# Retention and feed-forward on one core: more loads in flight, weight tiles of the beginning in two loads, and a new fixed order of the beginning

## The chip, the core and the metric

The kernel runs on one core of one Trainium2 chip. A core has five engines with an instruction stream each: TensorE (PE, with its weight loads as PEld), VectorE (DVE), ScalarE (ACT), GpSimd (POOL) and SyncE (SP), which here issues loads and stores only. Engines wait for each other and for DMA transfers by semaphores; each works through its own list in order. The metric is device time in microseconds (us). The kernel before takes 577.41 us, the median of three runs (575.93, 577.41, 577.48).

## The reference, cut to what matters

```python
# q, k, v: (4, 8, 768, 64)
for t in range(S):
    state = gamma * state + outer(k[t], v[t])        # per batch and head
    y[t] = scale * q[t] @ state
x = y.transpose(0, 2, 1, 3).reshape(3072, 512)
h = x @ w_in                                          # 512 x 2048
g = h * clip(h + 3, 0, 6) / 6
out = g @ w_out                                       # 2048 x 512
```

All inputs and the output are float32.

## The kernel before, in words

The 3072 tokens are 24 rows of 128 tokens, six to a batch. Four rows make a unit u of 512 tokens. The recurrence is computed in chunks of 64 tokens: scores of a row (k times q), weighed by a mask or a decay, times v, plus q times the state before, and the state is moved on by k times v. The result x of a unit is split into a high and a low part in a reduced float32 format, and so are the weights; a product is then three matmuls (high by high, high by low, low by high).

w_in is 16 tiles of 128 columns (j), each 128 x 512 in 64-bit floats, that is 512 KB. VectorE and ScalarE convert a tile to float32 in six steps and split it: a, b (bits of the exponent and the mantissa), e (ScalarE), q, f (the last that reads the loaded tile), w, and then u (high part, ScalarE) and v (low part, VectorE). A product tile hu.j is 12 matmuls of 128 x 512 (four k blocks by three). ScalarE (r) and VectorE (g) turn it into g, which goes to a buffer in HBM. When all units are through, a second phase multiplies by w_out with seven products in place of eight.

Up to the products of units 0 and 1 with all 16 tiles the order on each engine is written by hand: HEAD (L56), a list of words that `step` (L539 on) turns into instructions one by one. Each engine does its own words in this order; how the engines stand to each other is left to the semaphores. A word is a letter and numbers:

- Lr: the loads of row r (kt, qt, vn, kn of 256 KB each; from row 8 on also dq). F: the load of the next weight tile, F0 to F15 in this text. Both go to SyncE.
- O, N, Y, U (rows 0 to 3) and s, S, i, p, y (rows 4 to 7), P, Q (rows 8 on): scores, inner products, products with the state, sums of the state, all on TensorE. T: small table products. zn: n matmuls that fill time and whose result is not used.
- m: weighing the scores; x: the scaled result of a row; l: its low part (VectorE); X: its high part, A, B, J, K: copies of the state (ScalarE); c, d: decay of v (GpSimd for rows 0 to 5, ScalarE for 6 and 7); C: copies of the tables.
- a, b, e, q, f, w, u, v followed by the tile's number; hu.j: three of the 12 matmuls of a product tile; ru.j and gu.j.

SyncE's loads of the beginning go through `read` (L151). It keeps a list of loads in flight with their bytes per partition (2 KB for a row load, 4 KB for a weight tile). Where a new load would exceed the limit FLYING, the oldest are dropped from the list and the new one waits until the last dropped one has landed. This holds up to row 7; row 8 and later loads wait only for their buffers.

```python
    FLYING = 10 << 10
    ...
        while flying and sum(n for n, _ in flying) + size > FLYING:
            after = flying.pop(0)[1]
```

A weight tile is loaded into one of two buffers (tag st), so F of tile n also waits for step f of tile n - 2. The first product of unit 0 needs x of rows 0 to 3, of unit 1 x of rows 4 to 7.

Of the kernel before, what the change touches and what calls it, by code (L numbers as in the profile page):

```python
# [31 lines left out]
def retention_ffn(ctx: ExitStack, tc: tile.TileContext, qkv, w_in, w_out, dvs, dkc, dqc, dmc, tab, out, B, H, S, D):  # L32
# [23 lines left out]
    HEAD = """  # L56
        L0 L1 F L2 L3 L4 L5 F O0 T0 m0.0 c0 T1 C0 T2 m0.1 d0 C1 T3 C2 N0 C3 U0 x0 c1 T4 B0 d1 O1 C4 X0 l0 Y1 m1.0 U1
        m1.1 T5 B1 a0 N1 C5 e0 c2 b0 O2 d2 f0 x1 Y2 m2.0 X1 U2 m2.1 l1 B2 O3 q0 F L6 L7 c3 N2 d3 w0 Y3 u0 m3.1 m3.0 U3
        c4 x2 N3 B3 d4 v0 X2 s4 x3 p4 l2 X3 c5 m4 A4 d5 l3 S5 a1 y4 b1 e1 q1 B4 f1 F z1 h0.0 w1 p5 x4 u1 h0.0 m5 A5 X4
        v1 h0.0 c6 l4 S6 a2 d6 b2 y5 m6 h0.0 e2 x5 h0.1 q2 c7 h0.1 f2 F r0.0 p6 w2 d7 h0.1 g0.0 h0.1 a3 A6 u2 b3 S7 q3  # L60
        r0.1 v2 e3 y6 m7 X5 h0.2 f3 B6 h0.2 w3 p7 l5 i7 u3 x6 h0.2 A7 g0.1 y7 X6 v3 h0.2 B7 l6 h0.3 r0.2 x7 h0.3 g0.2
        X7 h0.3 a4 l7 L8 F h0.3 e4 b4 h1.0 r0.3 q4 h1.0 g0.3 h1.0 f4 F h1.0 w4 h1.1 r1.0 h1.1 u4 g1.0 h1.1 v4 h1.1
        h1.2 r1.1 Q8 g1.1 a5 h1.2 b5 K8 m8 e5 P9 q5 h0.4 J9 f5 F L9 h0.4 w5 h0.4 a6 u5 h0.4 b6 e6 q6 h1.2 r0.4 v5 h1.2
        f6 F h1.3 r1.2 w6 h1.3 a7 u6 h1.3 g1.2 e7 h1.3 b7 v6 h1.4 r1.3 f7 h1.4 g0.4 h1.4 g1.3 h1.4 q7 h1.5 r1.4 w7
        h1.5 a8 u7 g1.4 h1.5 e8 v7 h1.5 f8 Q9 L10 F r1.5 b8 q8 F g1.5 h1.6 K9 m9 X8 h1.6 w8 h1.6 l8 u8 h1.6 v8 h1.7
        r1.6 h1.7 g1.6 h1.7 h1.7 P10 r1.7 h1.8 J10 g1.7 h1.8 a9 b9 h1.8 e9 q9 h1.8 f9 F Q10 r1.8 w9 g1.8 u9 a10 h0.5
        K10 v9 X9 h0.5 m10 e10 h0.5 l9 h0.5 b10 q10 h0.6 r0.5 f10 F h0.6 g0.5 h0.6 w10 h0.6 a11 u10 b11 P11 r0.6 q11
        h1.9 J11 v10 e11 h1.9 g0.6 h1.9 f11 F h1.9 w11 h1.10 r1.9 a12 b12 h1.10 u11 g1.9 e12 h1.10 q12 h1.10 f12 F L11
        h0.7 r1.10 v11 h0.7 w12 h0.7 g1.10 u12 h0.7 a13 v12 e13 h0.8 b13 r0.7 h0.8 f13 h0.8 g0.7 q13 F h0.8 w13 h0.9
        r0.8 a14 h0.9 u13 g0.8 h0.9 e14 b14 q14 h0.9 f14 h0.10 r0.9 v13 h0.10 g0.9 h0.10 w14 h0.10 a15 u14 Q11 L12 b15  # L70
        r0.10 q15 e15 v14 h0.11 g0.10 K11 X10 h0.11 m11 l10 h0.11 f15 h0.11 w15 h0.12 r0.11 h0.12 u15 g0.11 h0.12 v15
        h0.12 h0.13 r0.12 h0.13 g0.12 h0.13 h0.13 h0.14 r0.13 h0.14 g0.13 h0.14 h0.14 h0.15 r0.14 h0.15 g0.14 h0.15
        h0.15 P12 r0.15 h1.11 J12 g0.15 h1.11 h1.11 h1.11 Q12 r1.11 g1.11 h1.12 m12 K12 X11 h1.12 l11 h1.12 h1.12
        h1.13 r1.12 h1.13 g1.12 h1.13 h1.13 h1.14 r1.13 h1.14 g1.13 h1.14 h1.14 h1.15 r1.14 h1.15 g1.14 h1.15 h1.15
        r1.15 g1.15
    """
# [827 lines left out]
```

## Time and profile before

| | before |
|---|---|
| median of three runs | 577.41 us |
| the profiled execution | 577.87 us, span 576.2 us |
| TensorE busy | 564.4 us, 98% of the span, 4930 matmuls |
| VectorE busy | 425.6 us, 74% |
| ScalarE busy | 242.6 us, 42% |
| GpSimd busy | 49.0 us, 9% |
| granted TensorE clock | full in every slice |
| chain that ended last | TensorE 91%, DMA 6%, VectorE 1% |

The span is the time between the first and the last instruction of the program in the profile; the execution's own time is a little more. Busy times are those in which an engine has an instruction at work; a busy TensorE can still be waiting inside, since the ends of matmuls are modelled. The chain is followed back from the last instruction, at each step to what released it. The whole DMA share of it lies in the beginning.

### The profile page before, as it was taken

To read this page: it belongs to the slowest core of one execution; us is meant where nothing else is said; L and a number is where in the kernel's file an instruction comes from. 1 tells how busy PE (TensorE), PEld (TensorE's weight loads), DVE (VectorE), ACT (ScalarE), POOL (GpSimd) and SP (SyncE) were. 2 spreads that over 40 slices of the span, in tenths; PEclk is the share of its full clock that TensorE was granted. 3 is DMA by queue.
4 is the path that set the end of the run, shared out by engine and by line. 5 is a ranking of instruction groups with operands and counts; after the bars stand their busy time and mean duration, and the time that the engine had idled before them with its cause. 6 is when DMAs were issued, how large, how long until landed. Compare 5 with 4: busy or idle time off the path is not lost.

```text
span 576.2 us, 12026 instructions
## 1 busy us (share of the span) xinstructions
PE 564.4 (98%) x4930; PEld 460.9 (80%) x4930; DVE 425.6 (74%) x594; ACT 242.6 (42%) x356; POOL 49.0 (9%) x58
## 2 busy tenths in 40 slices
PE   8789999999999999999999999999999999999997
PEld 6667888888888888888888888888888888888885
DVE  6688879942577767777737989689776798767881
ACT  3274445432444344444424654543335443444430
POOL 3301110121111111222000000000000000000000
PEclk9999999999999999999999999999999999999999
DMA  7986685844666666676443384665744757545611
GB/s 247 291 277 218 203 275 203 292 172 167 202 220 207 210 236 228 212 241 250 167 160 120 147 301 164 196 205 183 251 151 144 234 166 243 200 127 176 208 73 74
DMA packets 58467, 115.82 MB, mean 201 GB/s; under 512 B 5926, under 2 KB 6822, under 8 KB 58412
## 3 DMA queue, kind: packets, MB, share of 16 engines
q1 hardware_dynamic: 44144, 89.67, 47.8%
q10 hardware_dynamic: 14268, 25.38, 11.5%
q8 instruction: 39, 0.64, 0.5%
q14 instruction: 16, 0.13, 0.1%
HBM read 83.57 MB, written 31.46 MB: 200 GB/s over the span
## 4 chain that ended last, share of the span: by engine, by line
PE 91%; DMA 6%; DVE 1%; SPq 0%; issue 0%; DVEq 0%
PE h L497 45%; PE o L774 40%; DMA early<-in_qkv 4%; DMA st<-in_w_in 3%; PE uz L450 2%; PE sc L450 2%; PE y L450 2%; SPq L153 0%; DVE w L216 0%; DVE xr L601 0%; DVE x L216 0%; DVE g L508 0%; DVE we L177 0%; DVE wb L189 0%; DVE kept_v L718 0%
## 5 line engine op out<-in xcount | busy, mean ns | idle before, releaser
L497 PE MATMUL h<-x,w 128*128 128x512 f32 x1152 | 270.4, 393 | 0.5 <-DVE x L216 0.4
L497 PEld LDWEIGHTS h<-x,w 128*128 128x128 f32 x1152 | 214.0, 188 | 46.8 <-DVE x L216 0.8
L774 PE MATMUL o<-gc,w 128*128 128x512 f32 x1008 | 231.7, 391 | 0.0
L774 PEld LDWEIGHTS o<-gc,w 128*128 128x128 f32 x1008 | 188.9, 187 | 42.6
L504 ACT ACTIVATE g<-h,three 128x512 f32<-128x512 f32 x96 | 65.9, 688 | 109.2 <-PE h L497 82.2
L508 DVE SCALAR_TENSOR_TENSOR g<-g,h 128x512 f32<-128x512 f32 x96 | 65.8, 685 | 61.9 <-ACT g L504 61.6
L213 ACT ACTIVATE gc<-gv 128x1024 fp32r<-128x1024 f32 x48 | 50.9, 1060 | 62.2 <-PE o L774 58.1
L216 DVE TENSOR_TENSOR gc<-gv,gc 128x1024 fp32r<-128x1024 f32 x48 | 58.6, 1222 | 24.9 <-ACT gc L213 24.9
L213 ACT ACTIVATE gc<-spare 128x1024 fp32r<-128x1024 f32 x36 | 38.2, 1061 | 51.6 <-PE o L774 39.2
L216 DVE TENSOR_TENSOR gc<-spare,gc 128x1024 fp32r<-128x1024 f32 x36 | 44.0, 1221 | 11.2 <-ACT gc L213 11.1
L186 ACT ACTIVATE we<-we,ebias 128x512 int32<-128x512 int32 x32 | 23.0, 720 | 21.6 <-DVE we L177 21.6
L213 ACT ACTIVATE w<-ww 128x384 fp32r<-128x384 f32 (+2 forms) x34 | 18.6, 552 | 26.0 <-DVE ww L200 25.3
L454 ACT ACTIVATE state<-uz 128x256 f32<-128x256 f32 x41 | 15.6, 380 | 21.7 <-PE y L450 10.5
L200 DVE SCALAR_TENSOR_TENSOR ww<-wb,we 128x512 f32<-128x512 f32 x32 | 23.4, 733 | 0.9
L189 DVE SCALAR_TENSOR_TENSOR wb<-st,wb 128x512 f32<-128x512 uint32 x32 | 22.7, 708 | 0.7
L339 POOL TENSOR_TENSOR qs<-qt,dq 128x512 f32<-128x512 f32 x16 | 22.4, 1398 | 8.4 <-DMA dq<-in_decays_q 7.2
L194 DVE SCALAR_TENSOR_TENSOR we<-st,we 128x512 int32<-128x512 int32 x32 | 23.0, 720 | 0.0
L216 DVE TENSOR_TENSOR w<-ww,w 128x384 fp32r<-128x384 f32 (+2 forms) x34 | 21.0, 623 | 0.7 <-ACT w L213 0.5
L132 DVE TENSOR_TENSOR spare<-spare,gv 128x1024 f32<-128x1024 f32 x12 | 14.7, 1222 | 5.5 <-DMA gv<-gd 5.4
L450 PE MATMUL y<-qs,state 64*64 64x64 f32 x480 | 18.3, 222 | 0.0
L177 DVE TENSOR_SCALAR we<-st 128x512 int32<-128x512 int32 x32 | 13.6, 426 | 6.3 <-DMA st<-in_w_in 6.0
L450 PE MATMUL y<-am,vn 64*64 64x64 f32 x512 | 18.2, 219 | 0.0
(71 smaller groups left out, 408.1 us busy)
## 6 DMA issues: line engine op xcount, KB each, us to landing
gd<-g ACTq DMA_DIRECT2D x96, 256.0 KB, 2.9
gv<-gd SPq DMA_DIRECT2D x48, 512.0 KB, 4.9
gv<-gd SPq DMA_DIRECT2D x48, 256.0 KB, 3.1
st<-in_w_in SPq DMA_DIRECT2D x16, 512.0 KB, 4.5
st<-in_w_out SPq DMA_DIRECT2D x16, 512.0 KB, 5.9
early<-in_qkv SPq DMA_DIRECT2D x28, 256.0 KB, 4.2
kt<-in_qkv SPq DMA_DIRECT2D x16, 256.0 KB, 3.6
qt<-in_qkv SPq DMA_DIRECT2D x16, 256.0 KB, 4.0
```

The source lines that it names most:

```text
L186: nc.scalar.activation(out=t["e"], in_=t["e"], func=AF.Relu, scale=8.0, bias=ebias)
L189: nc.vector.scalar_tensor_tensor(out=t["b"].bitcast(F32), in0=lo.bitcast(U32), scalar=2.0**-32, in1=t["b"], op0=ALU.mult, op1=ALU.add)
L194: nc.vector.scalar_tensor_tensor(out=t["e"], in0=hi, scalar=-2147483648, in1=t["e"], op0=ALU.bitwise_and, op1=ALU.bitwise_or)
L200: nc.vector.scalar_tensor_tensor(out=t["w"], in0=t["b"].bitcast(F32), scalar=2.0**-20, in1=t["e"].bitcast(F32), op0=ALU.mult, op1=ALU.mult)
L213: nc.scalar.activation(out=hi, in_=src, func=AF.Copy)
L216: nc.vector.tensor_tensor(out=lo, in0=src, in1=hi, op=ALU.subtract)
L339: nc.gpsimd.tensor_tensor(out=t["qs"], in0=t["qt"], in1=d, op=ALU.mult)
L450: nc.tensor.matmul(out_, lhs, rhs, start=start, stop=True, skip_group_check=True)
L497: nc.tensor.matmul(h, t[:, o, a], xs[u][b][:, k], start=k + n == 0, stop=(k, n) == (NK - 1, 2), skip_group_check=True)
L504: return g, nc.scalar.activation(out=g, in_=h, func=AF.Relu, bias=three).ins
L508: ins = nc.vector.scalar_tensor_tensor(out=g, in0=g, scalar=6.0, in1=h, op0=ALU.min, op1=ALU.mult)
L774: nc.tensor.matmul(acc[i][h] if last else acc[i][:, h], w2c[j][:, RIGHT[i], x, h], gc[:, y, jj], start=j == 0 and n == 0, stop=j == NFP - ...
```

## The change

Three edits. The limit of bytes in flight goes from 10 KB to 14 KB per partition, that is from five row loads to seven (1.25 to 1.75 MB). In the beginning a weight tile is read by two loads of 2 KB per partition into the two halves of its buffer; the weight tiles of w_out in the later part are still one load. The list HEAD has another order; it has the same words, but for z1, which is now z4.

```diff
-    FLYING = 10 << 10
+    FLYING = 14 << 10
...
-        L0 L1 F L2 L3 L4 L5 F O0 T0 m0.0 c0 T1 C0 T2 m0.1 d0 C1 T3 C2 N0 C3 U0 x0 c1 T4 B0 d1 O1 C4 X0 l0 Y1 m1.0 U1
...
+        L0 F L1 L2 F L3 L4 L5 O0 c0 T0 m0.1 T1 d0 C0 T2 m0.0 C1 U0 C2 N0 B0 a0 b0 e0 q0 T3 T4 T5 f0 F L6 O1 c1 C3 Y1
...
-    def fetch(src):
+    def fetch(src, parts=1):
         st = wst.tile([P, src.shape[-1]], I64, tag="st", name=nm("st"), bufs=2)
-        read(st, src)
+        n = src.shape[-1] // parts
+        for i in range(parts):
+            read(st[:, i * n : (i + 1) * n], src[:, i * n : (i + 1) * n])
         return st
...
-                fetched.append(fetch(w_in[len(fetched)]))
+                fetched.append(fetch(w_in[len(fetched)], 2))
```

SyncE at the program's begin, before: early and kn are row loads (rows 0 and 1 in early_3, 2 and 3 in early_6, 4 and 5 in early_8, 6 and 7 in early_26; kn is the fourth load of an odd row), st is a weight tile, kt_66 on is row 8.

```order
L153 DMA early_3_134<-in_qkv 128x512 x7
L153 DMA kn_4_142<-in_qkv 128x512
L153 DMA st_5_144<-in_w_in 128x512
L153 DMA early_6_146<-in_qkv 128x512 x7
L153 DMA kn_7_154<-in_qkv 128x512
L153 DMA early_8_156<-in_qkv 128x512 x7
L153 DMA kn_9_164<-in_qkv 128x256
L153 DMA st_10_166<-in_w_in 128x512
L153 DMA st_25_340<-in_w_in 128x512
L153 DMA early_26_342<-in_qkv 128x512 x7
L153 DMA kn_27_350<-in_qkv 128x512
L153 DMA st_37_499<-in_w_in 128x512
```

Behind these rows come one more weight tile (st_48_613) and then row 8 (kt_66_802). Now, from the begin on, the same engine; early_9 is rows 4 and 5, early_21 rows 6 and 7:

```order
L153 DMA early_3_134<-in_qkv 128x512 x4
L153 DMA st_4_139<-in_w_in 128x256 x2
L153 DMA early_3_134<-in_qkv 128x512 x3
L153 DMA early_6_147<-in_qkv 128x512 x4
L153 DMA st_7_152<-in_w_in 128x256 x2
L153 DMA early_6_147<-in_qkv 128x512 x3
L153 DMA early_9_160<-in_qkv 128x512 x7
L153 DMA st_20_230<-in_w_in 128x256 x2
L153 DMA early_21_233<-in_qkv 128x512 x4
L153 DMA st_35_444<-in_w_in 128x256 x2
L153 DMA st_40_511<-in_w_in 128x256 x2
L153 DMA early_21_233<-in_qkv 128x512 x3
```

The single loads kn between these rows are left out. The first tile moved ahead of row 1, the second ahead of row 3, and the fourth and fifth ahead of row 7; three more tiles (st_52, st_63, st_75) now stand behind row 7 and ahead of row 8 (kt_76_856), where one stood before.

TensorE at the end of the attention of row 7, before: y_2 and uz are the last sums of that row, h_55 is the product tile h0.2, h_62 is h0.3, h_74 h1.0, h_78 h1.1 and h_80 h1.2; x_18 is x of unit 0, x_43 of unit 1; sc_125 is the scores of row 8.

```order
L450 MATMUL y_2_133<-early_26_342,state_60_754 64x64 x2
L497 MATMUL h_55_701<-x_18_241,w1_29_364 128x512 x3
L497 MATMUL h_62_782<-x_18_241,w1_29_364 128x512 x6
L497 MATMUL h_62_782<-x_18_241,w1_58_713 128x512 x6
L497 MATMUL h_74_824<-x_43_534,w1_29_364 128x512 x12
L497 MATMUL h_78_847<-x_43_534,w1_29_364 128x512 x12
L497 MATMUL h_80_866<-x_43_534,w1_29_364 128x512 x3
L450 MATMUL sc_125<-qt_67_804,kt_66_802 64x64 x16
```

Now: h_66 is h0.3, h_71 h0.4, h_74 h1.0, h_86 h1.1, h_91 h1.2; x_26 is x of unit 0, x_48 of unit 1.

```order
L452 MATMUL y_2_133<-early_21_233,state_65_786 64x64 x2
L499 MATMUL h_66_788<-x_26_311,w1_24_280 128x512 x3
L499 MATMUL h_66_788<-x_26_311,w1_55_636 128x512 x6
L499 MATMUL h_71_831<-x_26_311,w1_55_636 128x512 x9
L499 MATMUL h_74_848<-x_48_603,w1_24_280 128x512 x9
L499 MATMUL h_71_831<-x_26_311,w1_55_636 128x512 x3
L499 MATMUL h_74_848<-x_48_603,w1_24_280 128x512 x3
L499 MATMUL h_86_895<-x_48_603,w1_24_280 128x512 x12
L499 MATMUL h_91_920<-x_48_603,w1_24_280 128x512 x12
L452 MATMUL sc_125<-qt_77_858,kt_76_856 64x64 x16
```

A product tile of the fifth weight tile, h0.4, moved ahead of the first product tile of unit 1; before, it stood behind the scores of row 8. The scores of row 8 stand 48 products behind the begin of h0.4, and stood 27 behind the begin of h1.0.

VectorE at the same place, now: w1_55 is the low part of weight tiles (v), x_48 the low part of x of unit 1 (l), st_52 the sixth weight tile, g_64 and g_72 the results of h0.2 and h0.3.

```order
L510 SCALAR_TENSOR_TENSOR g_64_766<-g_64_766,h_57_653 128x512
L202 SCALAR_TENSOR_TENSOR ww_67_809<-wb_59_660,we_56_651 128x512
L603 TENSOR_TENSOR xr_69_816<-y_2_133,early_0_131 128x512
L179 TENSOR_SCALAR we_70_822<-st_52_626 128x512
L218 TENSOR_TENSOR w1_55_636<-ww_67_809,w1_55_636 128x4x128
L218 TENSOR_TENSOR x_48_603<-xr_69_816,x_48_603 128x4x128
L183 TENSOR_SCALAR wb_73_838<-st_52_626 128x512
L191 SCALAR_TENSOR_TENSOR wb_73_838<-st_52_626,wb_73_838 128x512
L510 SCALAR_TENSOR_TENSOR g_72_835<-g_72_835,h_66_788 128x512
L196 SCALAR_TENSOR_TENSOR we_70_822<-st_52_626,we_70_822 128x512
```

Before, the last low part of x of unit 1 (l7) stood behind the first step of tile 4 (a4), and the other steps of that tile behind l7; now all steps of tile 4 are ahead of l7, and step f of tile 5, which frees a buffer for the eighth tile, is the fifth instruction behind v of tile 4.

## Rows read from the trace of the kernel before

**Rows 1.** Busy time of each engine by stretches: the stretch, its length, busy time and instructions of PE, PEld, DVE, ACT and POOL, the granted clock, the DMA engines' busy share and GB/s.

```profile
2.00:42.00 40.00, 33.61 (x733) 26.25 (x731) 28.74 (x51) 17.93 (x44) 8.52 (x16) 1.00 0.88 285
6.16:50.46 44.30, 37.67 (x809) 29.34 (x807) 36.29 (x62) 21.01 (x50) 9.65 (x14) 1.00 0.84 276
60.00:140.00 80.00, 80.00 (x775) 65.18 (x774) 57.98 (x98) 34.22 (x60) 12.25 (x10) 1.00 0.67 230
```

**Rows 2.** The chain of waits in order of time, from the begin to 60 us: start, duration, what (early is a row load, st a weight tile).

```profile
2.65 4.37 DMA early<-in_qkv
7.04 5.90 DMA st<-in_w_in
...
25.71 4.11 DMA st<-in_w_in
...
35.30 4.45 DMA st<-in_w_in
...
39.84 0.43 DVE we L177
...
49.86 0.61 DVE x L216
50.52 6.19 PE h L497 x26
56.70 1.08 PE sc L450 x32
```

**Rows 3.** What SyncE's queue waited for, from 2 to 42 us: total us, times, longest.

```profile
SPq L153 <- DMA early<-in_qkv: 13.8, 19, 1.8
SPq L153 <- DMA st<-in_w_in: 6.8, 4, 3.2
```

**Rows 4.** Busy time by short stretches, columns as in rows 1: one with a full queue of loads, and three single microseconds.

```profile
3.00:8.00 5.00, 4.67 (x54) 3.07 (x55) 1.84 (x4) 1.08 (x2) 1.37 (x3) 1.00 1.04 342
13.00:14.00 1.00, 0.12 (x3) 0.00 (x0) 1.00 (x3) 0.52 (x1) 0.00 (x0) 1.00 0.19 68
...
25.00:26.00 1.00, 0.55 (x34) 0.45 (x32) 1.00 (x2) 0.39 (x1) 0.29 (x1) 1.00 0.50 130
...
38.00:39.00 1.00, 1.00 (x8) 0.84 (x5) 0.69 (x1) 1.00 (x5) 0.00 (x0) 1.00 0.80 152
```

**Rows 5.** VectorE's groups of instructions from 6.16 to 50.46 us: busy time, mean ns, and the idle time before them with what ended it. (The 3.6 us put down to "issue" lie before 6.16 us.)

```profile
L601 DVE TENSOR_TENSOR xr<-y,early 128x512 f32<-128x512 f32 x8 | 5.5, 687 | 1.2 <-PE y L450 1.2
...
L373 DVE TENSOR_TENSOR am<-sc,mask 128x512 f32<-128x512 f32 x8 | 5.1, 684 | 5.4 <-issue 3.6 <-PE y L450 1.9
...
L177 DVE TENSOR_SCALAR we<-st 128x512 int32<-128x512 int32 x5 | 2.2, 449 | 4.3 <-DMA st<-in_w_in 4.3
```

**Rows 6.** VectorE in order of time, 57 to 63 us, steps of two weight tiles: L177 is a, L181 b, L189 q, L194 f, L200 w, L216 v; start, duration.

```profile
57.39 0.42 DVE L177 TENSOR_SCALAR we<-st 128x512 int32<-128x512 int32 x1
57.73 0.42 DVE L181 TENSOR_SCALAR wb<-st 128x512 int32<-128x512 int32 x1
58.06 0.68 DVE L418 TENSOR_TENSOR am<-sc,cmask 128x512 f32<-128x512 f32 x1
58.66 0.68 DVE L189 SCALAR_TENSOR_TENSOR wb<-st,wb 128x512 f32<-128x512 uint32 x1
59.38 0.69 DVE L194 SCALAR_TENSOR_TENSOR we<-st,we 128x512 int32<-128x512 int32 x1
60.11 0.69 DVE L200 SCALAR_TENSOR_TENSOR ww<-wb,we 128x512 f32<-128x512 f32 x1
60.84 0.43 DVE L177 TENSOR_SCALAR we<-st 128x512 int32<-128x512 int32 x1
...
62.25 0.68 DVE L216 TENSOR_TENSOR w<-ww,w 128x512 fp32r<-128x512 f32 x1
62.85 0.68 DVE L194 SCALAR_TENSOR_TENSOR we<-st,we 128x512 int32<-128x512 int32 x1
```

**Rows 7.** TensorE: one filling matmul (z1, two records) and the first products behind it, in order of time; and 54 products in a row, from the chain.

```profile
27.91 0.70 PE L562 MATMUL h<-mask 128*128 128x256 f32 x2
28.25 1.06 PE L497 MATMUL h<-x,w 128*128 128x512 f32 x3
...
59.77 12.48 PE h L497 x54
```

**Rows 8.** Loads of a row from the ninth on: SyncE's issues of row 8 (its first) and at 60 us, in order of time; median time to landing of loads between 60 and 72 us; and GpSimd's scaling of row 8's kn.

```profile
37.57 0.42 SPq L153 DMA_DIRECT2D kt<-in_qkv  x1
...
60.10 0.33 SPq L153 DMA_DIRECT2D st<-in_w_in  x1
60.54 1.55 SPq L153 DMA_DIRECT2D kt<-in_qkv  x1
...
63.08 0.43 SPq L153 DMA_DIRECT2D am<-in_qkv  x1
...
64.14 0.65 SPq L153 DMA_DIRECT2D st<-in_w_in  x1
...
kt<-in_qkv SPq DMA_DIRECT2D x1, 256.0 KB, 5.5
...
am<-in_qkv SPq DMA_DIRECT2D x1, 256.0 KB, 6.2
...
46.11 1.21 POOL L335 TENSOR_TENSOR kn<-kn,ccst 128x512 f32<-128x512 f32 x1 [18.97 <-DMA kn<-in_qkv]
```

More of the change, by code (lines that the diff above doesn't have):

```diff
@@ L56, in retention_ffn @@
     HEAD = """
-        L0 L1 F L2 L3 L4 L5 F O0 T0 m0.0 c0 T1 C0 T2 m0.1 d0 C1 T3 C2 N0 C3 U0 x0 c1 T4 B0 d1 O1 C4 X0 l0 Y1 m1.0 U1
[L58 to L75, printed above, removed]
+        L0 F L1 L2 F L3 L4 L5 O0 c0 T0 m0.1 T1 d0 C0 T2 m0.0 C1 U0 C2 N0 B0 a0 b0 e0 q0 T3 T4 T5 f0 F L6 O1 c1 C3 Y1
+        d1 C4 m1.1 U1 m1.0 B1 w0 N1 c2 x0 u0 d2 O2 C5 X0 x1 U2 m2.0 X1 Y2 m2.1 B2 l0 N2 v0 c3 l1 O3 d3 x2 Y3 m3.0 X2
@@ new lines, in retention_ffn @@
+        m3.1 U3 l2 s4 B3 c4 a1 N3 b1 d4 e1 q1 p4 x3 m4 A4 X3 f1 F c5 S5 l3 d5 y4 w1 B4 a2 u1 b2 q2 e2 m5 f2 F L7 c6 z4
+        h0.0 v1 p5 d6 w2 S6 x4 u2 h0.0 a3 A5 m6 e3 h0.0 v2 X4 h0.0 f3 p6 r0.0 b3 h0.1 q3 F A6 h0.1 w3 h0.1 c7 l4 h0.1
+        g0.0 u3 a4 h0.2 r0.1 b4 S7 q4 e4 g0.1 d7 y6 m7 h0.2 x6 B6 y5 v3 X6 h0.2 x5 h0.2 l6 X5 p7 f4 F r0.2 i7 l5 A7
+        h0.3 g0.2 y7 w4 h0.3 B7 x7 u4 h0.3 a5 X7 v4 h0.3 e5 l7 h0.4 r0.3 b5 h0.4 q5 h0.4 g0.3 h1.0 f5 F L8 h1.0 w5
+        h1.0 a6 u5 b6 h0.4 e6 q6 h1.0 v5 r0.4 h1.1 f6 F r1.0 h1.1 g0.4 g1.0 h1.1 w6 h1.1 a7 h1.2 u6 b7 r1.1 q7 h1.2 e7
@@ new lines, in retention_ffn @@
+        v6 h1.2 g1.1 h1.2 f7 Q8 L9 F r1.2 w7 h1.3 a8 K8 g1.2 u7 P9 b8 e8 h1.3 m8 J9 h1.3 f8 h1.3 q8 F h1.4 v7 r1.3 w8
+        h1.4 g1.3 h1.4 u8 h1.4 v8 h1.5 r1.4 h1.5 g1.4 h1.5 a9 b9 e9 h1.5 q9 h1.6 r1.5 f9 F h1.6 w9 h1.6 g1.5 u9 h1.6
+        a10 v9 e10 h1.7 b10 r1.6 h1.7 f10 h1.7 g1.6 q10 h1.7 w10 h1.8 r1.7 a11 h1.8 u10 b11 e11 h1.8 q11 h1.8 g1.7 f11
+        Q9 L10 F F r1.8 v10 g1.8 h1.9 w11 K9 X8 h1.9 m9 u11 h1.9 l8 v11 h1.9 h1.10 r1.9 h1.10 g1.9 h1.10 h1.10 h1.11
+        r1.10 h1.11 g1.10 h1.11 a12 b12 h1.11 e12 q12 P10 r1.11 f12 h0.5 J10 g1.11 h0.5 w12 h0.5 a13 u12 h0.5 b13 e13
@@ new lines, in retention_ffn @@
+        q13 h0.6 r0.5 v12 h0.6 f13 h0.6 g0.5 h0.6 w13 h0.7 r0.6 h0.7 u13 g0.6 h0.7 v13 h0.7 Q10 L11 F F r0.7 g0.7 h0.8
+        m10 K10 X9 h0.8 l9 h0.8 h0.8 h0.9 r0.8 h0.9 g0.8 h0.9 h0.9 h0.10 r0.9 h0.10 g0.9 h0.10 a14 b14 e14 h0.10 q14
+        P11 r0.10 f14 h1.12 J11 w14 h1.12 g0.10 u14 h1.12 a15 v14 h1.12 e15 b15 Q11 L12 r1.12 f15 q15 g1.12 h1.13 X10
+        m11 h1.13 K11 l10 h1.13 w15 h1.13 u15 P12 r1.13 v15 h0.11 J12 g1.13 h0.11 h0.11 h0.11 h0.12 r0.11 h0.12 g0.11
+        h0.12 h0.12 h0.13 r0.12 h0.13 g0.12 h0.13 h0.13 h0.14 r0.13 h0.14 g0.13 h0.14 h0.14 h1.14 r0.14 h1.14 g0.14
@@ L76, in retention_ffn @@
+        h1.14 h1.14 h1.15 r1.14 h1.15 g1.14 h1.15 h1.15 Q12 r1.15 g1.15 h0.15 m12 X11 h0.15 K12 l11 h0.15 h0.15 r0.15
+        g0.15
     """
```

## The prediction

> **What bounds the kernel now.** I read the page first: TensorE is busy 98% of the span, so a change of the beginning can only win back time in which TensorE stands still. The busy times by stretch say where that is: between 6.16 and 50.46 us TensorE is busy 37.67 of 44.30 us, between 60 and 140 us 80.00 of 80.00 [rows 1]. Whatever comes after about 50 us follows TensorE back to back, in the time of its own instructions; the fixed list acts on the end through the moment at which this begins.
>
> The chain in order of time tells what sets that moment: one load after the other up to 39.75 us (35.30 + 4.45), then VectorE, which converts the fourth weight tile from 39.84 on and ends at 50.47 with the low part of the last x block of rows 4 to 7; at 50.52 TensorE starts the product tile h1.0 [rows 2]. The waits of SyncE's queue tell why the loads are slow: of 40 us it stood 13.8 waiting for a row load to land and 6.8 for a weight tile [rows 3]. That is the limit of loads in flight: a new load is issued when an old one lands, and a weight tile takes two of five places and gives them back together. The throughput shows the holes: 342 GB/s where the queue was full, but 68, 130 and 152 GB/s in the single microseconds at 13, 25 and 38 us [rows 4]; the mean over 2 to 42 us is 285 GB/s [rows 1].
>
> **A point at which both kernels can be compared.** Before h1.0 the old list has given TensorE the attention of rows 0 to 7 and 48 products (h0.0 to h0.3). The new list has given it exactly the same work when h0.4 starts, apart from three more filling matmuls (z4 for z1). From there each kernel has the same instructions left on TensorE. So the question is when h0.4 starts: earlier than 50.5 us is a gain of the difference, as long as TensorE waits nowhere later.
>
> Two floors for that moment. TensorE: 6.16 + 37.67 us of busy time + 3 x 0.34 us for the fills (27.91 to 28.25 [rows 7]) = 44.9 us. VectorE: h0.4 needs the fifth weight tile converted (v4), which h1.0 did not. Up to l7 the old list has 36.29 us of VectorE work after 6.16 us, and 44.30 - 36.29 = 8.0 us of idle time [rows 1]. Up to v4 the new list has five instructions more on balance: b, q, f, w, v of tile 4 and a of tile 5, less l7. From start to start these take 0.33, 0.72, 0.73, 0.73, 0.60 and 0.34, less 0.60 [rows 6]: 2.85 us. Floor: 6.16 + 36.29 + 2.85 = 45.3 us. VectorE is the later of the two, and what it idles is the whole question: with 5.2 us of idle time nothing is won, with more the change loses.
>
> **How much of the 8.0 us of idle time goes.** 4.3 us were waits of the first conversion step for a weight tile; 1.9 us were the score masks waiting in one place (row 3), 1.2 the x blocks waiting for TensorE [rows 5]. A quarter of a megabyte at 342 GB/s is 0.77 us, at 285 GB/s 0.92. With seven equal places that come free one by one I take 0.80, near the full queue, because what made the holes, two places freed at once behind a wait, is what goes. The fifth load landed at 7.02 us [rows 2]; so load number n lands at about 7.0 + 0.80 (n - 5). In the new order the first weight tile (numbers 5 and 6) lands at 7.8 us instead of 12.94; the second (16) at 15.8; row 3 (20) at 19.0; the third tile (30) at 27.0 instead of 29.8; the fourth and fifth (36 and 38) at 31.8 and 33.4, the fourth 8 us before the old 39.75; row 7 (42) at 36.6. VectorE's own work reaches the first step of tile 0 at 8.3, of tile 1 at 21, of tile 2 at 25.5 to 27, of tile 3 at 30 to 32 (the sum of its instructions, plus 0 to 2 us of idle time). So of the 4.3 us about 1.0 stays, at tiles 2 and 3. The wait of 1.9 us halves, since row 3 comes some 1 us earlier. Idle: 8.0 - 3.3 - 0.9 = 3.8 us. I leave the other hand-overs as they were: the list is tighter, so some get shorter and others appear. Then v4 is done at 45.3 + 3.8 = 49.1 us, 1.4 us before the old 50.5. TensorE's floor lies 4.2 us below that, so the three fills cost nothing; if VectorE came down to its floor they would cost up to 1.0 us.
>
> **What is later afterwards.** The loads of row 8 were issued from 37.57 us on and used at 56.70 [rows 2, 8]: no wait. Now the eighth weight tile stands ahead of them on SyncE and waits for step f of tile 5 (two buffers), in VectorE's list the fifth instruction behind v4: 0.60 + 0.33 + 0.72 + 0.60 + 0.73 = 3.0 us later, at 52.1. The burst of row 8 follows h0.4 by 48 products at 0.231 us (12.48 / 54 [rows 7]), 11.1 us: at 60.2, and needs the scaled kn after 1.08 us of scores, at 61.3. Its kn is the sixth load from there. If they land as the first loads did (the fifth 6.2 us after the first issue, one more 0.8) it is there at 59.1, scaled by GpSimd in 1.21 us at 60.3: no wait. If they land as at 60 us (a tile first, then a row: issue at 63.08 plus 6.2, so 9.2 us after 60.10 [rows 8]) it is scaled at 62.5: 1.2 us of wait. I take 0.4, nearer to the first loads, whose form and order these have.
>
> The row at 60 us also shows that loads issued close together each take longer: 5.5 and 6.2 us to land [rows 8] against 4.37 for the fifth load of the program [rows 2]. The Trainium skill (DMA: Bandwidth & Descriptors, section Latency and other measured facts) has a rule that speaks against a deeper queue: access to HBM takes 0.2 us on average and 2 us at high load, and the fixed part of a load grows with it. The trace agrees in direction, with the 1.8 us between these two rows. By that rule the wait at row 8 is at its upper end, and the sum is that of the third rival below; without it, the sum is the one here.
>
> Splitting a tile into two loads adds 16 issues of 0.33 to 0.65 us on SyncE. In the first 40 us it waits for landings for 20.4 us [rows 3], which covers them; behind v4 the one extra issue ahead of row 8 is in the 0.4 us.
>
> At the end of the list the last burst (row 12) now stands one product tile before the steady part, where it stood four before it. The new x block needs a copy and a subtraction after it, about 0.6 us each with their hand-overs 1.6 us, and the tile takes 2.77: covered; if not, under 1 us.
>
> **Sum.** 1.4 gained - 0.4 = 1.0 us. The profiled execution took 577.87 us around its span of 576.2, which is 0.46 above the median of the three runs: 576.9 by the one, 576.4 us by the median 577.41, and this is my forecast. A difference below 0.3% (1.7 us) can't be told from none here. Own range of this case: 575.0 to 577.7.
>
> **Rivals.**
> - The loads run ahead and VectorE idles only 1.5 to 2 us. Then v4 is done at 47, the lead is 3.4 us, 0.2 stay at row 8: 574.2 us. For it: 4.3 + 1.9 = 6.2 us of the idle time hang on loads [rows 5], and both floors are at 45. Against it: each list that hands over between four engines has shown hops, 3.7 us of them here.
> - The five tiles. By the point of comparison VectorE must have converted five tiles rather than four, and its idle time stays at 8.0 us, because what it waits for are the rows' chains through TensorE, GpSimd and ScalarE and not the tiles: h0.4 starts at 53.3, 2.8 us late: 580.2 us, slower. It decides from 5.2 us of idle time on. For it: 2.85 us more work is certain, the savings are not, and the tiles now push rows 2 to 7 back by two to six loads. Against it: 4.3 us are plainly the tiles' own.
> - Row 8 takes the lead back. Lead 1.4, but its kn lands 9.2 us after the tile's issue and the wait is 1.2 to 1.4 us: 577.3 us, no change.
> - The deeper queue does nothing. Transfers are already busy 0.88 of 2 to 42 us [rows 1]; if the packets only get slower, tiles come as early as the order puts them, but row 7 comes late: idle time about 5 us, 577.2 us, no change.
>
> **Chances.** Forecast 0.42, loads ahead 0.25, five tiles 0.13, row 8 takes it back 0.12, the queue does nothing 0.08. Faster by over 0.3%: all of the second and about a third of the first, 0.38. Slower: the five tiles, 0.12. Within: the rest, 0.50. The range reaches from inside the case of the loads ahead to inside that of the five tiles: 574.0 to 578.6 us.
>
> **What would show it.** Right: throughput from 3 to 36 us without the holes, SyncE's waits for tiles near 1 us; the first conversion step of the fourth tile near 32 us instead of 39.84; VectorE idle about 4 us between 6 us and v4; h0.4 near 49 us; TensorE without idle time from there, but for some tenths before the uz products of row 8. Wrong: VectorE idle over 5 us before v4, idle TensorE behind h0.4 other than at row 8, or loads that land more than 0.92 us apart in a full queue.

## The result and the profile after

The changed kernel takes 579.94 us, the median of seven runs (578.53 to 582.1), against 577.24 us for the kernel before (seven runs, 575.93 to 577.48): a ratio of 1.0054, interval 1.0039 to 1.0069. It is slower by 3.1 us by the ratio (2.7 by the medians), where 576.4 us was forecast, and lies outside the range. One execution further below, of the kernel with one fill, took 627.39 us at a granted clock of 0.85 and is left out of its median and ratio. The profiled execution took 581.75 us around a span of 580.0, 3.9 us above that of the kernel before (577.87). It is one of the three longest of the seven (581.24 to 582.1; the other four took 578.53 to 579.94), so its rows show more loss than the median has. Lines behind the changed functions carry numbers that are 2 higher than before (L177, step a, is now L179; L194, step f, is L196; L454, the state copy K, is L456).

Busy time by stretches, columns as in [rows 1], for the changed kernel; the first three and the one at 13 us answer to [rows 1] and [rows 4], with the second stretch drawn out to the end of v4:

```profile
2.00:42.00 40.00, 34.26 (x626) 27.07 (x625) 30.03 (x52) 16.76 (x40) 9.73 (x16) 0.96 0.82 283
6.16:52.20 46.04, 40.12 (x845) 31.85 (x838) 38.52 (x67) 22.45 (x52) 8.71 (x12) 0.96 0.72 249
60.00:140.00 80.00, 78.30 (x830) 63.57 (x832) 51.20 (x89) 32.80 (x56) 11.65 (x10) 1.00 0.64 224
10.00:20.00 10.00, 8.23 (x194) 6.84 (x192) 9.40 (x16) 2.66 (x6) 4.40 (x6) 1.00 1.04 375
13.00:14.00 1.00, 0.60 (x10) 0.60 (x12) 0.95 (x2) 0.03 (x2) 0.63 (x1) 1.00 1.04 358
...
30.00:40.00 10.00, 10.00 (x145) 7.81 (x138) 6.18 (x12) 7.31 (x21) 0.00 (x0) 0.83 0.51 176
...
60.00:70.00 10.00, 8.30 (x107) 6.53 (x106) 7.46 (x14) 4.41 (x8) 2.28 (x2) 1.00 0.99 337
...
70.00:145.00 75.00, 75.00 (x753) 61.13 (x752) 45.92 (x79) 29.95 (x51) 9.37 (x8) 1.00 0.61 212
```

Read in order: the hole at 13 us is filled (358 GB/s where 68 stood in [rows 4]). VectorE idles 46.04 - 38.52 = 7.5 us up to v4. From 30 to 40 us the granted clock is 0.83, where [rows 1] had 1.00. And behind 60 us TensorE, which had no idle time there in [rows 1], loses 80.00 - 78.30 = 1.70 us, all of it before 70 us: from 70 to 145 us it is busy 75.00 of 75.00.

What SyncE's queue waited for from 2 to 42 us, as in [rows 3]:

```profile
SPq L153 <- DMA early<-in_qkv: 6.8, 17, 1.0
SPq L153 <- DVE we L196: 6.2, 2, 3.6
SPq L153 <- DVE wb L191: 4.7, 1, 4.7
SPq L153 <- DMA st<-in_w_in: 1.7, 3, 1.2
```

The waits for landings fell from 13.8 and 6.8 us to 6.8 and 1.7. In their place stand 10.9 us of waits for VectorE: a weight tile can't be fetched before a buffer of the two is converted. VectorE's groups from 6.16 to 52.20 us, columns as in [rows 5]:

```profile
L603 DVE TENSOR_TENSOR xr<-y,early 128x512 f32<-128x512 f32 x8 | 5.5, 687 | 4.9 <-PE y L452 4.8
L375 DVE TENSOR_TENSOR am<-sc,mask 128x512 f32<-128x512 f32 x8 | 5.1, 679 | 4.5 <-PE sc L452 4.5
...
L196 DVE SCALAR_TENSOR_TENSOR we<-st,we 128x512 int32<-128x512 int32 x5 | 3.4, 684 | 1.4 <-ACT we L188 1.4
L179 DVE TENSOR_SCALAR we<-st 128x512 int32<-128x512 int32 x6 | 2.9, 488 | 0.0
```

VectorE no longer waits for a weight tile at all (4.3 us in [rows 5]), nor ahead of the masks of row 3 (1.9): the 4.5 us of the mask row all stand before the first mask, and only 0.9 of them lie behind 6.16 us. But it waits 4.8 us for TensorE's y (1.2 before) and 1.4 for ScalarE's step e (nothing before). In order of time (start, duration, instruction, the wait before it), the first mask, and the longest wait for y, which stands ahead of the first step of the fourth tile:

```profile
7.07 1.29 DVE L375 TENSOR_TENSOR am<-sc,mask 128x512 f32<-128x512 f32 x2 [4.47 <-PE sc L452]
...
36.07 0.69 DVE L603 TENSOR_TENSOR xr<-y,early 128x512 f32<-128x512 f32 x1 [2.29 <-PE y L452]
36.68 0.42 DVE L179 TENSOR_SCALAR we<-st 128x512 int32<-128x512 int32 x1
```

TensorE is what came late there, and the chain in order of time says why (start, duration, what):

```profile
8.88 0.42 DVE we L179
...
27.98 1.81 issue
29.79 0.33 PE uz L452 x3
30.14 3.61 PE h L564 x8
33.75 0.69 PE h L499 x3
...
57.57 6.18 DMA gd<-g
...
63.83 0.35 ACT g L506
...
64.71 0.73 ACT we L188
...
67.42 0.38 ACT state L456
...
67.84 0.27 PE uz L452 x2
```

There are two places. At 27.98 us TensorE stands 1.81 us in the middle of y4 and waits for nothing that the profile shows ("issue"); then the fills z4 take 3.61 us for eight matmuls, at half the granted clock. At 57.57 us a product's store is issued; it lands 6.18 us later and ScalarE's r1.1 waits for it. The next store is issued behind r1.1, r1.2 waits for that one, and row 8's state copy (67.42), which stands behind r1.2 on ScalarE, comes late for TensorE. TensorE's side of it, waits from 60 to 70 us:

```profile
ACT g L506 <- DMA gd<-g: 4.2, 2, 2.8
PEld uz L452 <- ACT state L456: 2.1, 1, 2.1
...
PE uz L452 <- ACT state L456: 1.7, 1, 1.7
```

VectorE in order of time dates the end of v4:

```profile
51.52 0.68 DVE L218 TENSOR_TENSOR w<-ww,w 128x512 fp32r<-128x512 f32 x1
```

It ends at 52.20 us. TensorE has no idle time there. Behind y7, the last sums of row 7, it runs nine products of h0.3 and then h0.4 in one row:

```profile
50.41 3.94 PE L499 MATMUL h<-x,w 128*128 128x512 f32 x16
```

At some 0.23 us a product h0.4 begins near 52.6 us; h1.0 began at 50.52 [rows 2]. That is 2.1 us, with the 1.70 us behind 60 us 3.8 of the 3.9. TensorE came to h0.4 some 0.4 us after v4 had ended and did not wait for it.

### The profile page after: what moved, and what is told of

The parts are those of the page before. It is cut to its first block, busy times and chain, and to the rows that moved or that the text cites. A ratio compares the mean times of both kernels' runs of the same rounds, so it can differ in the third digit from the quotient of the medians.

```text
span 580.0 us, 12046 instructions
## 1 busy us (share of the span) xinstructions
PE 567.4 (98%) x4936; PEld 463.6 (80%) x4936; DVE 422.7 (73%) x594; ACT 244.3 (42%) x356; POOL 48.5 (8%) x58
## 4 chain that ended last, share of the span: by engine, by line
PE 93%; DVE 4%; DMA 1%; issue 1%; ACT 0%; ACTq 0%; DVEq 0%
PE h L499 44%; PE o L776 40%; PE uz L452 3%; PE y L452 3%; PE sc L452 3%; DMA gd<-g 1%; PE idle L292 1%; DVE am L375 1%; PE h L564 1%; DVE xr L603 0%; DVE x L218 0%; DVE wb L191 0%; DVE we L196 0%; DVE early L559 0%; DVE am L420 0%
## 5 line engine op out<-in xcount | busy, mean ns | idle before, releaser
L218 DVE TENSOR_TENSOR gc<-spare,gc 128x1024 fp32r<-128x1024 f32 x36 | 43.9, 1219 | 10.9 <-ACT gc L215 10.8
L456 ACT ACTIVATE state<-uz 128x256 f32<-128x256 f32 x41 | 15.6, 381 | 23.9 <-PE y L452 15.6
L196 DVE SCALAR_TENSOR_TENSOR we<-st,we 128x512 int32<-128x512 int32 x32 | 22.0, 688 | 1.7 <-ACT we L188 1.7
L337 POOL TENSOR_TENSOR kn<-kn,ccst 128x512 f32<-128x512 f32 x8 | 8.6, 1079 | 116.9 <-DMA kn<-in_qkv 56.8
```

The lines of the kernel that those rows point to most:

```text
L196: nc.vector.scalar_tensor_tensor(out=t["e"], in0=hi, scalar=-2147483648, in1=t["e"], op0=ALU.bitwise_and, op1=ALU.bitwise_or)
L218: nc.vector.tensor_tensor(out=lo, in0=src, in1=hi, op=ALU.subtract)
```

## The experiments

Two places were suspected for the 3 us. The first lies ahead of h0.4: more loads in flight may hold up the loads of TensorE's own instructions, and three more fills follow at half the clock. The second is row 8, whose loads the new list issues late and in the middle of others. (The letters of theories in the expectations change their meaning from run to run.) Each kernel ran 6 to 12 times between runs of the kernel before on the same chip; ratios are to those, and the median of the kernel before lay between 576.85 and 577.37 us.

**Row 8 first.** In the changed list, row 8's loads ahead of the eighth weight tile.

```diff
-        h0.3 g0.2 y7 w4 h0.3 B7 x7 u4 h0.3 a5 X7 v4 h0.3 e5 l7 h0.4 r0.3 b5 h0.4 q5 h0.4 g0.3 h1.0 f5 F L8 h1.0 w5
+        h0.3 g0.2 y7 w4 h0.3 B7 x7 u4 h0.3 a5 X7 v4 h0.3 e5 l7 L8 h0.4 r0.3 b5 h0.4 q5 h0.4 g0.3 h1.0 f5 F h1.0 w5
```

> The changed kernel with the loads of row 8 ahead of the eighth weight tile (L8 moved in front of F7 in the list). Theory A: they are issued at about 48.5 us instead of 55.9, land before row 8's burst and before the stores of the product tiles crowd with them; the wait of 1.9 us between the scores of row 8 and the sums behind them goes; time 1.5 to 2 us under the changed kernel, about 578 us. Theory C (that wait is of ScalarE's own order and has nothing to do with the loads): it stays, no change.

Measured: 577.54 us, ratio 1.0000 (0.9989 to 1.0012), 2.4 us under the changed kernel. The windows of this kernel:

```profile
60.00:70.00 10.00, 10.00 (x114) 7.96 (x113) 9.73 (x18) 5.97 (x11) 0.38 (x1) 1.00 0.90 296
```

TensorE's wait behind 60 us is gone. But the edit moves both the landing of kn and the crowd of loads around the store, so it doesn't tell yet which of the two the wait hung on.

**State copy first.** In the changed list, only row 8's state copy on ScalarE is put ahead of r1.2; the loads stay late.

```diff
-        v6 h1.2 g1.1 h1.2 f7 Q8 L9 F r1.2 w7 h1.3 a8 K8 g1.2 u7 P9 b8 e8 h1.3 m8 J9 h1.3 f8 h1.3 q8 F h1.4 v7 r1.3 w8
+        v6 h1.2 g1.1 h1.2 f7 Q8 L9 F K8 r1.2 w7 h1.3 a8 g1.2 u7 P9 b8 e8 h1.3 m8 J9 h1.3 f8 h1.3 q8 F h1.4 v7 r1.3 w8
```

> The changed kernel with one word moved: the state copy K8 ahead of r1.2 on ScalarE. If the wait behind the scores of row 8 is this copy standing behind r1.2, which waits for the store of an earlier product tile that lands in 6.2 us among the loads of row 8: most of the 1.9 us goes, 578.0 to 578.6 us. If the loads of row 8 themselves are late (the scaled kn and qs): at most 0.4 us goes, 579.4 to 580 us.

Measured: 577.9 us, ratio 1.0009 (0.9995 to 1.0024), 2.0 us under the changed kernel. ScalarE of this kernel in order of time (start, duration, instruction, the wait before it):

```profile
60.09 0.69 ACT L506 ACTIVATE g<-h,three 128x512 f32<-128x512 f32 x1 [2.67 <-DMA gd<-g]
...
61.72 0.38 ACT L456 ACTIVATE state<-uz 128x256 f32<-128x256 f32 x1
62.84 0.69 ACT L506 ACTIVATE g<-h,three 128x512 f32<-128x512 f32 x1 [0.73 <-DMA gd<-g]
```

r1.1 still waits 2.67 us for its store, which took 6.0 us among the same loads; only the copy no longer stands behind r1.2, and TensorE no longer waits:

```profile
60.00:70.00 10.00, 10.00 (x114) 8.26 (x114) 8.00 (x14) 5.90 (x10) 2.85 (x4) 1.00 0.97 320
```

That alone takes away nearly all that the move of the loads took. The wait was the state copy's place on ScalarE behind waits for stores, not the landing of kn. The kernel before shows the same from the other side. There, too, ScalarE waits for a store among a row's loads (row 9), with no copy right behind it, and TensorE loses nothing (80.00 of 80.00 in [rows 1]):

```profile
68.90 0.69 ACT L504 ACTIVATE g<-h,three 128x512 f32<-128x512 f32 x1 [2.95 <-DMA gd<-g]
```

**Both.** The two edits above together.

```diff
-        h0.3 g0.2 y7 w4 h0.3 B7 x7 u4 h0.3 a5 X7 v4 h0.3 e5 l7 h0.4 r0.3 b5 h0.4 q5 h0.4 g0.3 h1.0 f5 F L8 h1.0 w5
+        h0.3 g0.2 y7 w4 h0.3 B7 x7 u4 h0.3 a5 X7 v4 h0.3 e5 l7 L8 h0.4 r0.3 b5 h0.4 q5 h0.4 g0.3 h1.0 f5 F h1.0 w5
...
-        v6 h1.2 g1.1 h1.2 f7 Q8 L9 F r1.2 w7 h1.3 a8 K8 g1.2 u7 P9 b8 e8 h1.3 m8 J9 h1.3 f8 h1.3 q8 F h1.4 v7 r1.3 w8
+        v6 h1.2 g1.1 h1.2 f7 Q8 L9 F K8 r1.2 w7 h1.3 a8 g1.2 u7 P9 b8 e8 h1.3 m8 J9 h1.3 f8 h1.3 q8 F h1.4 v7 r1.3 w8
```

> The changed kernel with both cures for the wait at row 8 at once: row 8 loaded ahead of the eighth fetch (as in the run with row 8 first) and row 8's state copied on ScalarE ahead of the product tile r1.2. If the two cures take away one and the same wait, together they give no more than either alone: 577.5, within 0.4 us. If each removes a part of its own (loads that are late, and a copy that stands behind a store), they add: 577.54 less another 1 to 2 us, 575.5 to 576.5, and the new list would be no dearer than the old one.

Measured: 578.07 us, ratio 1.0014 (0.9999 to 1.0029). They don't add: it is one wait. In its profile TensorE waits 1.9 us ahead of h0.4 for a step x (and 1.4 us for another at 117.7 us), and the chain leads there from row 7's load, which was issued behind the fifth weight tile:

```profile
32.33 6.57 DMA early<-in_qkv
...
40.50 0.68 ACT g L506
41.20 0.69 DVE g L510
41.89 0.60 DVE am L420
42.49 0.61 DVE xr L603
43.14 0.68 PE y L452 x16
```

**Row 7 first.** To test that: row 8 first, and row 7 right behind row 6, where the list before has it.

```diff
-        L0 F L1 L2 F L3 L4 L5 O0 c0 T0 m0.1 T1 d0 C0 T2 m0.0 C1 U0 C2 N0 B0 a0 b0 e0 q0 T3 T4 T5 f0 F L6 O1 c1 C3 Y1
+        L0 F L1 L2 F L3 L4 L5 O0 c0 T0 m0.1 T1 d0 C0 T2 m0.0 C1 U0 C2 N0 B0 a0 b0 e0 q0 T3 T4 T5 f0 F L6 L7 O1 c1 C3 Y1
...
-        m3.1 U3 l2 s4 B3 c4 a1 N3 b1 d4 e1 q1 p4 x3 m4 A4 X3 f1 F c5 S5 l3 d5 y4 w1 B4 a2 u1 b2 q2 e2 m5 f2 F L7 c6 z4
+        m3.1 U3 l2 s4 B3 c4 a1 N3 b1 d4 e1 q1 p4 x3 m4 A4 X3 f1 F c5 S5 l3 d5 y4 w1 B4 a2 u1 b2 q2 e2 m5 f2 F c6 z4
...
-        h0.3 g0.2 y7 w4 h0.3 B7 x7 u4 h0.3 a5 X7 v4 h0.3 e5 l7 h0.4 r0.3 b5 h0.4 q5 h0.4 g0.3 h1.0 f5 F L8 h1.0 w5
+        h0.3 g0.2 y7 w4 h0.3 B7 x7 u4 h0.3 a5 X7 v4 h0.3 e5 l7 L8 h0.4 r0.3 b5 h0.4 q5 h0.4 g0.3 h1.0 f5 F h1.0 w5
```

> The changed kernel with row 8 loaded ahead of the eighth fetch (as in the run with row 8 first) and row 7 loaded right behind row 6, where the list before has it, in place of behind the fifth fetch, whose issue waits for step f of tile 2. With row 8 first alone the time was 577.5, 1.4 us above the old list with the same limit and split (576.2). If those 1.4 us are row 7's late landing (with both cures its landing of 6.57 us at 38.9 us stood at the head of the chain, and TensorE then waited 2.3 us for step x), they go: 576.2, 575.7 to 576.8, with TensorE busy 9.6 or more of the 10 us from 40 to 50 (8.1 to 9.1 in the runs with row 8 or its copy first). If they are the new list's order of tile steps and its fills, or the stops of TensorE for its instructions, moving row 7 gives nothing: 577.3 to 577.9.

Measured: 577.49 us, ratio 1.0015 (1.0002 to 1.0029). It gains nothing over row 8 first (1.0000), though from 40 to 50 us TensorE is now busy 9.32 us (9.12 with row 8 first, 8.10 with both cures). Row 7's landing headed one profiled chain; it is not what the new list costs in most executions.

**The old list with the new limit and the split.** The kernel before, with only the other two parts of the change.

```diff
-    FLYING = 10 << 10
+    FLYING = 14 << 10
...
-    def fetch(src):
+    def fetch(src, parts=1):
...
-                fetched.append(fetch(w_in[len(fetched)]))
+                fetched.append(fetch(w_in[len(fetched)], 2))
```

> The old list with the limit of 14 KB and the tiles in two loads. Theory A: loads land earlier as in the changed kernel, but TensorE's gaps without a wait (0.78 and 0.98 us before) grow to 1.5 to 2 us each; no wait at row 8, since its loads stand behind tile 4 only; time 576 to 578 us. Theory B: the loads are all that the old list lacks: 573 to 575 us.

Measured: 576.16 us, ratio 0.9983 (0.9972 to 0.9994): faster than both kernels, by little against the kernel before. So the new list costs 579.94 - 576.16 = 3.8 us, and the other two parts gain 1.2.

**Each of those two alone.** The limit:

```diff
-    FLYING = 10 << 10
+    FLYING = 14 << 10
```

> The kernel before with the limit of 14 KB alone (old list, tiles in one load). Theory A (the limit alone brings the loads earlier, and part of it is given back where TensorE waits for its instructions): 576.0 to 576.8 us, a gap without a wait of over 1.2 us on TensorE between 25 and 30 us. Rival (a tile that takes two places at once is what makes the holes, so the limit alone does little): within 0.4 us of the kernel before.

Measured: 576.53 us, ratio 0.9979 (0.9964 to 0.9994). The executions fall into two groups, four of 573.58 to 574.65 us and eight of 576.2 to 577.47; no run shows why. And the split:

```diff
-    def fetch(src):
+    def fetch(src, parts=1):
...
-                fetched.append(fetch(w_in[len(fetched)]))
+                fetched.append(fetch(w_in[len(fetched)], 2))
```

> The kernel before with weight tiles in two loads alone (old list, limit of 10 KB). Theory A (places free one by one, the queue no longer drains behind a tile): loads up to 0.5 us earlier, 576.9 to 577.3 us. Rival (two issues and two landings per tile cost as much as they give): 577.4 to 578 us.

Measured: 576.79 us, ratio 0.9992 (0.9980 to 1.0004). The limit alone is the gain; the split by itself can't be told from nothing, nor can what it adds to the limit (576.16 against 576.53).

**A higher limit still**, on the old list.

```diff
-    FLYING = 10 << 10
+    FLYING = 18 << 10
```

> The kernel before with the limit at 18 KB per partition (2.25 MB) in place of 10 KB, nothing else. If the gain of 14 KB (0.8 us) comes from loads that land sooner, and is not used up, 18 KB gives as much again or a little more: 575.5 to 576.3. If 14 KB already fills the memory's rate (375 GB/s over 10 to 20 us in the changed kernel), 18 KB gives the same as 14 KB: 576.5. If deeper loads hold up TensorE's own instructions, which come through the same queues, it is back at 577.3 or above.

Measured: 576.88 us, ratio 0.9993 (0.9978 to 1.0008): no more than 14 KB and not clear of no gain. TensorE's stops from 23 to 32 us that no wait explains, one profile each; first this kernel, then 14 KB on the old list, then the kernel before (total us, times, longest):

```profile
PE uz L450 <- issue: 3.0, 1, 3.0
```

```profile
PE uz L450 <- issue: 1.5, 1, 1.5
```

```profile
PE uz L450 <- issue: 1.4, 2, 0.8
```

The longest stop grows with the limit here. But with the split alone, at 10 KB, the longest is 1.3 us and the total 2.1, so one profile each doesn't settle it.

**The changed kernel with the old limit.**

```diff
-    FLYING = 14 << 10
+    FLYING = 10 << 10
```

> The changed kernel with the old limit of 10 KB per partition; list and split kept. Theory A: the gap of TensorE that no wait explains (at 27.8 us, 2.03 us long) shrinks to 0.8 us or less, since fewer packets of loads stand ahead of the fetch of instructions; the loads land later by 1 to 3 us; the wait at row 8 stays at 1 to 2 us; time 578 to 580 us. Theory B (the deeper queue only helps): the gap stays, everything up to h0.4 gets later by 1 to 3 us, time 580.5 to 583 us.

Measured: 582.32 us, ratio 1.0085 (1.0066 to 1.0103). The stop of TensorE at 28 us is gone from this profile (from 23 to 32 us it waits only 1.4 us, for a mask), and yet the kernel is 2.4 us slower than with 14 KB. The deeper queue is a gain for the new list too. That the stop went can't be put to the limit: in the other six profiles of the new list with 14 KB it is 0.4 us or less as well. So the stop is no steady cost of the new list, and the loss is not the deeper queue's.

**One fill in the changed list**, as before.

```diff
-        m3.1 U3 l2 s4 B3 c4 a1 N3 b1 d4 e1 q1 p4 x3 m4 A4 X3 f1 F c5 S5 l3 d5 y4 w1 B4 a2 u1 b2 q2 e2 m5 f2 F L7 c6 z4
+        m3.1 U3 l2 s4 B3 c4 a1 N3 b1 d4 e1 q1 p4 x3 m4 A4 X3 f1 F c5 S5 l3 d5 y4 w1 B4 a2 u1 b2 q2 e2 m5 f2 F L7 c6 z1
```

> The changed kernel with one filling matmul instead of four (z1 for z4). Theory A (TensorE stood still before the fills, partly 2.03 us for its own instruction stream, its clock fell to half, and the fills then take 3.05 us instead of about 1.4; and 1.9 us are lost at row 8): the fills cost at most 0.9 us, h0.4 starts 1.5 to 2.5 us earlier, the time is 577.5 to 578.5 us where the clock falls. Theory B (the order of the five tiles on VectorE sets the moment of h0.4, the fills lie beside a wait): h0.4 moves by under 0.5 us, the time stays within 0.5 us of the changed kernel.

Measured: 579.1 us, ratio 1.0043 (1.0025 to 1.0061), 0.8 us under four fills, with intervals that overlap. The same edit together with row 8 first:

```diff
-        h0.3 g0.2 y7 w4 h0.3 B7 x7 u4 h0.3 a5 X7 v4 h0.3 e5 l7 h0.4 r0.3 b5 h0.4 q5 h0.4 g0.3 h1.0 f5 F L8 h1.0 w5
+        h0.3 g0.2 y7 w4 h0.3 B7 x7 u4 h0.3 a5 X7 v4 h0.3 e5 l7 L8 h0.4 r0.3 b5 h0.4 q5 h0.4 g0.3 h1.0 f5 F h1.0 w5
```

> The changed kernel with the loads of row 8 ahead of the eighth tile and one fill instead of four. If fills and row 8 are separate costs: row 8's part of 2.4 us goes, and the fills give 0.5 to 1 us where they stood on the path: 576.3 to 577.2 us, h0.4 near 49 us. If the fills lie beside a wait (the median with one fill was only 0.2 us under the changed kernel): 577.3 to 577.8 us, as with the loads of row 8 alone.

Measured: 577.98 us, ratio 1.0010 (0.9992 to 1.0028), 0.4 us above the four fills with row 8 first. And four fills in the old list at 14 KB:

```diff
-        c4 x2 N3 B3 d4 v0 X2 s4 x3 p4 l2 X3 c5 m4 A4 d5 l3 S5 a1 y4 b1 e1 q1 B4 f1 F z1 h0.0 w1 p5 x4 u1 h0.0 m5 A5 X4
+        c4 x2 N3 B3 d4 v0 X2 s4 x3 p4 l2 X3 c5 m4 A4 d5 l3 S5 a1 y4 b1 e1 q1 B4 f1 F z4 h0.0 w1 p5 x4 u1 h0.0 m5 A5 X4
```

> The kernel before with the limit at 14 KB and the fill at tile 4 as four fills (z4) in place of one, as the new list has it: sizes the step 'three fills cost nothing' on the old list. If the fills stand in a hole of TensorE's, as the prediction had it, the time is that of 14 KB alone, 576.5 or 0.3 below it, with fewer executions at a granted clock under 0.998 (3 of 12 with one fill). If TensorE is wanted as soon as the fills begin, three more fills of 8 matmuls at 0.2 us would cost at most some 0.7 to 1 us: 577.2 to 577.5.

Measured: 577.14 us, ratio 1.0002 (0.9987 to 1.0017), 0.6 us above one fill, with intervals that overlap. On the new list the fills cost -0.4 to 0.8 us, on the old one perhaps 0.6. None of the three is clear of nothing, all are within the 1.0 us set down for them at most, and none makes up the 3 us.

## Why the prediction was wrong

**The step that failed is the one on what is later afterwards.** Of row 8 it priced only the landing of kn, at 0.4 us. That price was not too low: GpSimd scaled kn at 63.47 us in 1.04,

```profile
63.47 1.04 POOL L337 TENSOR_TENSOR kn<-kn,ccst 128x512 f32<-128x512 f32 x1 [38.16 <-DMA dq<-in_decays_q]
```

ready at 64.51, and no row shows TensorE waiting for it. What the step left out is what row 8's loads do to others. SyncE issued them at the time of a product's store (start, duration, issue):

```profile
55.09 0.80 SPq L153 DMA_DIRECT2D st<-in_w_in  x2
55.94 0.43 SPq L153 DMA_DIRECT2D kt<-in_qkv  x1
...
57.37 0.43 SPq L153 DMA_DIRECT2D kn<-in_qkv  x1
```

The store, issued at 57.57, took 6.18 us, where the shortest of the five stores from 50 to 70 us took 2.0; that is the same slowing of transfers which the prediction read from [rows 8] and applied to kn alone. ScalarE's r1.1 and r1.2 waited 2.8 and 1.4 us for stores, the state copy came behind r1.2, and TensorE stood 1.70 us. The two runs that cure this in different ways give back 2.4 and 2.0 us, and together no more. The rule that was weighed, that the fixed part of a transfer grows with the load on HBM (the Trainium skill, DMA: Bandwidth & Descriptors, Latency and other measured facts), agrees in direction with the 6.18 against 2.0 us (which part of it is the fixed one no run shows) and was put on the wrong transfer. And a slow store is not enough: the run with the copy first still waits 2.67 us for its store, and is 2.0 us faster. The rival that row 8 takes the lead back put 1.2 to 1.4 us at the right place, not far from the 1.70, but by the landing of kn: its size was luck.

**The lead of 1.4 us was not there, because the hand-overs that were left as they were grew.** The sum of VectorE's work held (36.29 + 2.85 = 39.1 forecast, 38.52 measured). Of its idle time 3.8 us were forecast up to v4; the profiled execution has 7.5, and v4 ends at 52.20 instead of 49.1. The waits for tiles and for row 3's masks went wholly, 6.2 us where 4.2 were taken off. The other 1.8 us (8.0 less 6.2) were left as they were and became 7.5: 4.8 for y, 1.4 for step e, 0.9 ahead of the first mask, the rest in tenths. In four other profiles of this list, with the wait at row 8 cured and the clock full up to there, v4 ends at 50.06 (row 8 first), 48.62 (copy first), 50.21 (both) and 49.16 us (row 7 first). The last of them:

```profile
48.48 0.68 DVE L218 TENSOR_TENSOR w<-ww,w 128x512 fp32r<-128x512 f32 x1
```

VectorE idled 5.4, 4.2, 5.5 and 4.45 us in them (window less busy time, as 43.00 - 38.55 in the last). So 3.8 was low by 0.4 to 1.7 there, and by 3.7 where TensorE stopped at 27.98 and the clock fell behind it. For the profiled execution the sum of 1.4 gained less 0.4 should have read 2.1 lost and 1.7 more.

Nor was v4 the gate that the prediction made of it ("VectorE is the later of the two"). In all eight profiles of the new list TensorE came to h0.4 some 0.4 us after v4 had ended, behind y7 and nine products. On VectorE, too, v4 stands behind a wait for y7, 1.0 to 1.1 us in each. What sets the moment is the chain of row 7, which goes to and fro between the two engines, and not VectorE's sum alone.

The rival of the five tiles named the right condition (idle time above 5.2 us), and in the profiled execution it was met: by hand-overs, as the rival had it, 2.3 us of them behind a stop of TensorE that it had not. Its 580.2 us lies near the measured 579.94 by luck, since it has nothing of the loss at row 8.

**Loads 0.80 us apart:** right up to the fourth tile. From 10 to 20 us 375 GB/s were moved, which is 0.70 us for a quarter megabyte. The first tile's step a began at 8.88 (8.3 forecast); the fourth tile landed at 31.9 us (31.8 forecast). Its step a still began at 36.68 instead of 30 to 32, because VectorE waited 2.3 us for y4 ahead of it, and not for the tile. But the fifth tile landed at 36.2 us (33.4 forecast): behind the third fetch no load was late for want of a place in flight, SyncE waited for a buffer. The issue times:

```profile
27.04 6.25 SPq L153 DMA_DIRECT2D st<-in_w_in  x4
33.33 1.38 SPq L153 DMA_DIRECT2D early<-in_qkv  x3
```

The fourth and fifth tiles were issued from 27.04 to 33.3, each behind a step f, and row 7 behind them. The forecast counted loads from the start at 0.80 us each and never set them against the two buffers, which [rows 3] could not yet show.

**Tile waits and mask waits:** the 4.3 us for tiles went wholly (3.3 forecast), and so did the 1.9 us for the masks of row 3 (half of it forecast).

**Three fills cost nothing:** not refuted on the median, by three comparisons of -0.4, 0.8 and 0.6 us with overlapping intervals. In the profiled execution they ran at half the clock and stood on the chain with 3.61 us, which no term foresaw.

**The split's issues and the end of the list are covered:** right. The split alone is 0.9992, so no cost of it can be seen, and TensorE is busy 75.00 of 75.00 us from 70 us on and 15.00 of 15.00 from there to 160 us, past the last burst.

**The rival that the queue does nothing** is wrong: the limit alone is worth 0.7 us on the old list by the medians (1.2 by the ratio) and 2.4 us on the new.

What stays open: with row 8 cured the new list still stands at 1.0000 to 1.0015, the old list with the same limit at 0.9979 to 0.9983, so it costs another 1 to 2 us in the median. Row 7's landing was tried and isn't it; the fills are at most a part. In the four profiles with row 8 cured and the clock full h0.4 begins at 49.0 to 50.6 us; at 14 KB on the old list h1.0 begins at 48.6 to 49.7 in three. The two ranges overlap, with one profile of each kernel, so it is not shown whether the rest lies ahead of that point.

## What to carry to other kernels

When loads are moved to a later place, price what they do to the transfers that are in flight there, the stores among them, and follow from each such transfer what waits behind it in its engine's order: here a copy of 0.38 us stood behind a wait for a store that had nothing to do with it. A queue of loads made deeper is a gain only until the next limit: with 14 KB and the new list SyncE waited 10.9 us for the two buffers of a weight tile. Count those before the places in flight. And try the parts of a change apart: the limit alone was faster than either kernel.
